# Gate weights and the first event blocks loaded into memory that the packing leaves, other weights in a set order behind the blocks

## The chip, the cores and the metric

The kernel runs on 1 core of one Trainium2 chip. The metric is the device time of one execution in microseconds (us), the median of 3 runs. The engines are PE (matrix products), DVE (vector), ACT (activations, casts, copies), POOL (general element work) and SP, which issues every DMA of this kernel.

## What is computed

Three stages in a row, on 8 batches of 576 tokens with 512 features, in float32:

```
p_packed = softmax(p k^T / 8) v ;  x = softmax(q p_packed^T / 8) p_packed      # packing, 8 heads of 64
x  = sum over the 2 best of 4 experts e:  w_e * (causal softmax attention of x wq_e, x wk_e, x wv_e) @ wo_e
xk = mu_k * x + (1 - mu_k) * x_prev ;  xr = mu_r * x + (1 - mu_r) * x_prev
k  = max(xk @ w_k, 0) ;  r = 1 / (1 + exp(-(xr @ w_r))) ;  out = r * ((k * k) @ w_v)
```

The last stage (512 features in, 1024 hidden, 512 out) is done on three tokens at once: an "event" is 3 tokens, there are 1536 events, in 6 blocks of 256.

## The kernel before

**First stretch, to about 460 us.** For each batch the packing and the four experts are computed. The pieces (`front`, `values`, `project`, `soft`, `turn`, `pair_out`) are steps with a due time in a hand-written table (`FRONT_T` to `OUT_LAG`); all steps of all batches are sorted by due time and written out in that order, and a scheduler sets each engine's order from there by priorities (`PR`). L459 finds a softmax row's maximum on DVE, L463 is its exp on ACT, L479 and L486 transpose the result on PE, L188 copies it back, L524 multiplies by the values, L541 adds the experts (`cb`), L195 makes `dt` on POOL and L558 writes it as events to the DRAM tensor `dscr`, 16 times in all. Between them the weights `w_r`, `w_k`, `w_v` are folded for events and written to DRAM (`wscrr`, `wscrk`, `vscr`).

**Weights for the last stage.** A float32 product runs as three products of a high and a low half, so each weight is loaded (L726), its high half copied (POOL or ACT), and the low half found by a subtraction (L728) on DVE or POOL. There are 4 such planes each of r (the gates' weight), k0, k1, and v.

**Second stretch, the gates, about 456 to 533 us.** For each of six blocks `load_block` reads 1 MB of events (L768, tile `dl`), POOL copies the high half (`dh`, L184) and DVE subtracts (L770). `rstage` does 128 of the 256 events: 24 matmuls of 128x512 on PE (L792) into two `one` banks and a `big` pair of PSUM, `p` copied by ACT (L798), three DVE operations that combine the parts (L775, L776, L777), the sigmoid on ACT (L801), and the gates written to DRAM (`rscr`, L803). PSUM holds two such half-blocks. `dl`, `dh` and `rr` have two buffers each. In before all six blocks, with the gates, are due after the last `pair_out`.

**Third stretch, from 533 us.** For each block `kstage` (L814), the square and its halves (L822 to L827, L195), and `vstage` (L847), with L852 multiplying by the gates. It starts with block 4, whose `dl` and `dh` are still there.

**Memory.** `swap_w` closes the right-hand pools (`bt`, `wa`, `ld`, `fr`, `dv`) after the last batch's `project` and puts there pool "ba" (k0, the blocks) and "bw" (r). `swap_end` closes the left-hand pools (`sm`, `vp`, `ex`) after the last `pair_out` and puts k1 and v there. A load into such memory waits for the last reader of what lay there. All DMAs are issued by SP, one after the other; one that waits holds up the ones behind it.

Of the kernel before, what the change touches and what calls it, by code (L numbers as in the profile page):

```python
# [33 lines left out]
V_END = -11.02  # L34
WA_AT = -24.33
R_AT, R_STEP = 0.2, 2.0
# [8 lines left out]
PR = {"front": 0, "values": -100, "project": 0, "soft": 0, "turn": 0, "out": 100, "fold": 0, "v": -70, "k": 0}  # L45


def f32(ap):
    return ap.bitcast(F32)
# [3 lines left out]
def kernel(  # L53
# [85 lines left out]
    if True:  # L139
        bt_cm, bt = pool("bt", 1, "right")  # L140
# [6 lines left out]
        ex_cm, ex = pool("ex", 2, "left")  # L147

# [562 lines left out]
        def swap_w():  # L711

            close(bt_cm, wa_cm, ld_cm, fr_cm, dv_cm)
            cms["ba"], pools["a"] = pool("ba", 1, "right")
            weight("k0", "a")
            cms["bw"], pools["w"] = pool("bw", 1, "right")
            weight("r", "w")
# [6 lines left out]
        def load_part(h, l, src, eng):  # L724

            nc.sync.dma_start(f32(l), src)  # L726
            evac(eng[0], h, f32(l))
            (nc.vector if eng[1] == "V" else nc.gpsimd).tensor_sub(l, f32(l), f32(h))  # L728

        def load_weight(n_, eng):  # L730
            h, l = wres[n_]
            for j in range(NS):
                load_part(h[:, j], l[:, j], wscr[n_][:, j], eng)
                yield

        def swap_end():
            close(sm_cm, vp_cm, ex_cm)
            cms["bb"], pools["b"] = pool("bb", 1, "left")
            weight("k1", "b")
            for _ in load_weight("k1", "AV"):  # L740
                pass
# [4 lines left out]
            for j in range(0, NFT, 2):  # L746
                load_part(h[:, j : j + 2], l[:, j : j + 2], vscr[:, j : j + 2], "AP")
# [15 lines left out]
        def load_block(i):  # L763
# [4 lines left out]
            nc.sync.dma_start(f32(dl), dscr[:, :, e0 : e0 + EB])  # L768
# [106 lines left out]
        swap = max(last, U * (B - 1) + max(PROJ_T) + 0.05)  # L875
        add("k", call(swap_w), [swap])
        for x, n_ in enumerate(("r", "k0")):
            add("k", load_weight(n_, "PV"), even(swap + 0.1 + 8 * x, swap + 8.1 + 8 * x, 4))

        for i in range(NEB):  # L880
            due = U * B + OUT_LAG[2] + R_AT + R_STEP * i
            add("k", call(load_block, i), [due])
            for x, t0 in enumerate(range(0, EB, P)):
                add("k", call(rstage, i, t0), [due + 0.5 + x * R_STEP / 2])
        add("k", call(swap_end), [U * B + OUT_LAG[2] + 0.1])
# [80 lines left out]
```

## Time and profile before

| what | value |
| --- | --- |
| median of 3 runs (lowest, highest) | 870.78 us (870.21, 874.48) |
| the profiled execution's own time | 875.03 us |
| span of its profile, mean granted PE clock | 873.2 us, 0.988 |
| PE matmuls busy | 812.5 us, 93% |
| DVE, ACT, POOL busy | 572.1 (66%), 363.2 (42%), 401.6 (46%) us |
| DMA moved | 113.71 MB, mean 130 GB/s |

PE is the busiest engine, so time is lost where PE has nothing to do or runs at the lower clock. The span is cut into stretches, and for each the busy time of PE tells how much is lost there; in the stretches that are short of work the engine's own rows tell after which instruction it waited, in square brackets with the instruction or DMA that released it. `<-DMA x<-y` is a transfer. An issue row on SP is where the DMA was started, not where its data were there.

### The profile page before, as it was taken

What the parts mean: (1) busy time and instruction counts of PE and PEld (TensorE: products, weight loads), DVE (VectorE), ACT (ScalarE), POOL (GpSimd) and SP (SyncE); (2) the same over time, 40 slices, a digit from 0 to 9 for tenths busy, and PEclk for the clock granted to TensorE, in tenths of its full rate; (3) what the DMA queues carried; (4) which work ended last, traced back from release to release, by engine and by line L of the source; (5) the groups of instructions that cost most, each with busy time, mean ns of one, the idle gap of its engine ahead of it and who ended that gap; (6) DMA issues with size and microseconds to landing.
All of it is one profiled execution on the core that took longest, in us unless ns stands there. A gap on an engine that the chain in (4) does not pass through costs nothing. (4 is left out here: it accounts for less than half of the span.)

```text
span 873.2 us, 15003 instructions
## 1 busy us (share of the span) xinstructions
PE 812.5 (93%) x5408; PEld 676.2 (77%) x5408; DVE 572.1 (66%) x1297; ACT 363.2 (42%) x916; POOL 401.6 (46%) x539
## 2 busy tenths in 40 slices
PE   5699979999999998988789699999999999999998
PEld 3486948779687795767667589998889888898896
DVE  3899696976959789998954675554454644544342
ACT  2347636576655765766576233211212112021120
POOL 6678476584865755546632510432423223232230
PEclk9899999999999999999999899999999999999999
DMA  9754552735536364333817564023121131110301
GB/s 308 235 158 158 149 163 89 205 108 148 170 106 196 101 181 175 117 108 111 254 59 265 209 255 181 1 85 109 49 88 57 54 141 49 73 73 1 145 2 72
DMA packets 65546, 113.71 MB, mean 130 GB/s; under 512 B 9920, under 2 KB 44224, under 8 KB 65472
## 3 DMA queue, kind: packets, MB, share of 16 engines
q1 hardware_dynamic: 65472, 112.75, 39.7%
q8 instruction: 43, 0.70, 0.3%
q14 instruction: 31, 0.25, 0.1%
HBM read 69.74 MB, written 33.55 MB: 118 GB/s over the span
## 5 line engine op out<-in xcount | busy, mean ns | idle before, releaser
L195 POOL TENSOR_TENSOR kk<-y,kk 128x768 fp32r<-128x768 f32 x48 | 89.5, 1864 | 222.1 <-ACT kk L827 222.1
L847 PE MATMUL one<-wvh,kk 128*128 128x512 f32 x576 | 187.7, 393 | 0.1
L847 PEld LDWEIGHTS one<-wvh,kk 128*128 128x128 f32 x576 | 107.7, 188 | 22.4 <-DVE rr L852 0.5
L847 PE MATMUL one<-wvl,kk 128*128 128x512 f32 x288 | 113.1, 393 | 0.0
L463 ACT ACTIVATE ms<-ms,nb 64x64 f32<-64x64 f32 (+4 forms) x160 | 89.4, 559 | 46.6 <-DVE nb L459 44.5
L775 DVE TENSOR_TENSOR y<-big,p 128x256 f32<-128x256 f32 x48 | 20.3, 424 | 116.8 <-POOL kk L195 100.5
L827 ACT CAST kk<-y 128x768 fp32r<-128x768 f32 x48 | 40.1, 836 | 131.3 <-DVE y L825 94.8
L188 ACT COPY tb<-one 64x128 f32<-64x128 f32 (+5 forms) x208 | 65.9, 356 | 17.5 <-PE one L479 15.3
L822 ACT COPY p<-big 128x256 f32<-128x256 f32 x48 | 17.9, 373 | 128.3 <-PE big L814 105.9
L479 PE MATMUL one<-ident,ms 128*128 128x128 f32 x320 | 54.4, 282 | 11.0 <-DVE nb L459 6.0
L847 PEld LDWEIGHTS one<-wvl,kk 128*128 128x128 f32 x288 | 54.2, 188 | 10.3
L459 DVE CUSTOM_DVE_ANT_0 ms<-one,mstrip 64x64 f32<-64x64 f32 (+3 forms) x128 | 51.4, 420 | 11.3 <-PE one L447 7.0
L524 PE MATMUL one<-tb,vg 128*64 128x320 f32 (+4 forms) x448 | 56.2, 362 | 0.9 <-ACT tb L188 0.7
L479 PEld LDWEIGHTS one<-ident,ms 128*128 128x128 f32 x320 | 37.4, 141 | 21.7 <-issue 11.1
L524 PEld LDWEIGHTS one<-tb,vg 128*64 128x64 f32 x448 | 38.0, 137 | 18.2 <-ACT tb L188 2.9
L594 POOL TENSOR_TENSOR dcx<-dcx,dcu 128x256 f32<-128x256 f32 x40 | 30.8, 770 | 44.3 <-DVE dcu L588 18.3
L852 DVE TENSOR_TENSOR rr<-one,rr 128x512 f32<-128x512 f32 x36 | 23.1, 685 | 41.8 <-PE one L847 41.8
L825 DVE SCALAR_TENSOR_TENSOR y<-y 128x768 f32<-128x768 f32 x48 | 47.9, 998 | 1.6
L447 PE MATMUL one<-ks,qs 128*128 128x64 f32 (+3 forms) x128 | 39.6, 335 | 3.4 <-ACT ks L397 1.0
L184 POOL TENSOR_SCALAR dh<-dl 128x2048 fp32r<-128x2048 f32 x10 | 22.7, 2266 | 42.0 <-DMA dl<-dscr 42.0
L814 PE MATMUL big<-dl,wk0h 128*128 128x256 f32 x192 | 39.6, 282 | 0.0
L770 DVE TENSOR_TENSOR dl<-dl,dh 128x2048 fp32r<-128x2048 f32 x10 | 27.8, 2782 | 17.8 <-POOL dh L184 17.8
(178 smaller groups left out, 2147.8 us busy)
## 6 DMA issues: line engine op xcount, KB each, us to landing
dl<-dscr SPq DMA_DIRECT2D x10, 1024.0 KB, 6.2
kT<-in_k_dram SPq DMA_DIRECT2D x16, 576.0 KB, 4.2
qT<-in_q_dram SPq DMA_DIRECT2D x16, 576.0 KB, 5.7
rscr<-rr SPq DMA_DIRECT2D x12, 768.0 KB, 4.0
rr<-rscr SPq DMA_DIRECT2D x12, 768.0 KB, 4.3
out_dram<-rr SPq DMA_DIRECT2D x11, 768.0 KB, 3.3
vn<-in_v_dram SPq DMA_DIRECT2D x16, 512.0 KB, 4.6
dscr<-dt SPq DMA_DIRECT2D x16, 384.0 KB, 3.7
```

Of the source, the lines that this page charges most:

```text
L188: nc.scalar.copy(o, x)
L195: nc.gpsimd.tensor_tensor(o, x, y, op=op)
L447: nc.tensor.matmul(ps[:, po : po + kn], qs[:, i * P : i * P + P], keys[:, ko : ko + kn], start=x == 0, stop=x == 1,)
L459: nc.vector.tensor_tensor_reduce(halves(mv) if last else mv, sv, halves(mk) if last else mk, op0=ALU.add, op1=ALU.min, scale=-SC, scalar=3 ...
L463: nc.scalar.activation(mv, mv, AF.Exp, bias=nb[p0:], scale=-1.0, accum_out=bat["sums"][p0:, i, e : e + 1],)
L479: nc.tensor.transpose(ps[:, at + j * P : at + (j + 1) * P], ms[:, j * P : (j + 1) * P], ident)
L524: nc.tensor.matmul(av[64 * ee : 64 * ee + 64, qo - lo : hi - lo], vg[:, j, HD * (2 * ep + ee) : HD * (2 * ep + ee + 1)], tslice(tabs[ee], ...
L594: nc.gpsimd.tensor_add(f32(t["x"]), f32(t["x"]), f32(t["u"]))
L814: nc.tensor.matmul(ps[:, o : o + EB], wpart("k0" if f < 4 else "k1", s, wx, t)[:, f % 4 * P : f % 4 * P + P], dx[:, NS * t + s, :], start= ...
L825: nc.vector.scalar_tensor_tensor(y, y, 0.0, y, op0=ALU.max, op1=ALU.mult)
L827: nc.scalar.copy(kk[:, 0], y)
L847: nc.tensor.matmul(ps, kk[:, a, x, t0 : t0 + P], wres["v"][b][:, f, :], start=n == 0, stop=n == 3 * NFT - 1,)
```

## The change

`bt`, which lives to the end, moves to the left side, so that the right side is free as soon as `values` of the last batch and its last weight folding are done (`V_END`): `swap_w` is now due some 14 table units earlier, and it places only the blocks' pool and r. The loads of r are due 8 units after it, those of blocks 0 and 1 at 14 and 15, and their gates at 22 and 28, all inside the last batch's experts. `load_part` and `load_block` get a flag `late`, which pins the DMA in program order on SP's queue. k0 moves to the left side with k1 and v; the three load after the last `pair_out`, at set times among the gates of blocks 2 to 5, pinned. The high half of k0 is made by ACT in place of POOL. Gates and their block loads have a kind of their own with the same priority as before.

```diff
+WR_AT = 8.0
+R_LOAD, R_RUN = [14.0, 15.0], [22.0, 28.0]
+E_R = "PV"
+W_AT = [2.2, 4.2, 5.2]
...
-        bt_cm, bt = pool("bt", 1, "right")
...
+        bt_cm, bt = pool("bt", 1, "left")
...
-            close(bt_cm, wa_cm, ld_cm, fr_cm, dv_cm)
+            close(wa_cm, ld_cm, fr_cm, dv_cm)
             cms["ba"], pools["a"] = pool("ba", 1, "right")
-            weight("k0", "a")
             cms["bw"], pools["w"] = pool("bw", 1, "right")
             weight("r", "w")
...
-        def load_part(h, l, src, eng):
-
-            nc.sync.dma_start(f32(l), src)
+        def load_part(h, l, src, eng, late=False):
+
+            dma = nc.sync.dma_start(f32(l), src)
+            if late:
+                tc.keep_in_program_order(dma)
...
         def swap_end():
-            close(sm_cm, vp_cm, ex_cm)
+
+            close(sm_cm, vp_cm, ex_cm, bt_cm)
             cms["bb"], pools["b"] = pool("bb", 1, "left")
-            weight("k1", "b")
-            for _ in load_weight("k1", "AV"):
-                pass
+            for n_ in ("k0", "k1"):
+                weight(n_, "b")
+                for _ in load_weight(n_, "AV", True):
+                    yield
...
-                load_part(h[:, j : j + 2], l[:, j : j + 2], vscr[:, j : j + 2], "AP")
+                load_part(h[:, j : j + 2], l[:, j : j + 2], vscr[:, j : j + 2], "AP", True)
+                yield
...
-            nc.sync.dma_start(f32(dl), dscr[:, :, e0 : e0 + EB])
+            dma = nc.sync.dma_start(f32(dl), dscr[:, :, e0 : e0 + EB])
+            if late:
+                tc.keep_in_program_order(dma)
...
-        swap = max(last, U * (B - 1) + max(PROJ_T) + 0.05)
+        swap = max(last, U * (B - 1) + V_END + 0.1)
         add("k", call(swap_w), [swap])
-        for x, n_ in enumerate(("r", "k0")):
-            add("k", load_weight(n_, "PV"), even(swap + 0.1 + 8 * x, swap + 8.1 + 8 * x, 4))
-
+        add("k", load_weight("r", E_R, True), even(swap + WR_AT, swap + WR_AT + 4.0, 4))
+        end = U * B + OUT_LAG[2] + 0.1
         for i in range(NEB):
-            due = U * B + OUT_LAG[2] + R_AT + R_STEP * i
-            add("k", call(load_block, i), [due])
+            early = i < len(R_LOAD)
+            add("gates", call(load_block, i, early), [swap + R_LOAD[i] if early else end + i])
             for x, t0 in enumerate(range(0, EB, P)):
-                add("k", call(rstage, i, t0), [due + 0.5 + x * R_STEP / 2])
-        add("k", call(swap_end), [U * B + OUT_LAG[2] + 0.1])
+                add("gates", call(rstage, i, t0), [(swap + R_RUN[i] if early else end + i + 1.5) + 0.05 * x])
+        add("k", swap_end(), [end + W_AT[j // 4] + 0.01 * j for j in range(12)])
```

The lines of the changed kernel lie 3 to 9 further down than those of before. The engines' orders differ from the last batch's `project` to the end of the gates; in the first 400 us and in the third stretch they are alike.

**First place: SP and POOL at the start of the gates.** Each `dl` or `dh` with a number is one block's; in before 6431 is block 2 and 6506 block 3. SP before, from the last `dscr` write:

```order
L558 DMA dscr<-dt_6241 128x4x192
L726 DMA wk1l<-wscrk_91 128x1024 x4
L726 DMA wvl<-vscr 128x1024 x4
L803 DMA rscr<-rr_6314 128x1536
L768 DMA dl_6431<-dscr 128x8x256
L803 DMA rscr<-rr_6349 128x1536
L768 DMA dl_6506<-dscr 128x8x256
L803 DMA rscr<-rr_6389 128x1536
L803 DMA rscr<-rr_6424 128x1536
```

SP after, where 6382 is block 2, 6408 block 3 and 6483 block 4; `wvl` stands four rows further down, behind block 5:

```order
L775 DMA dl_6011<-dscr 128x8x256
L561 DMA dscr<-dt_6109 128x4x192
L775 DMA dl_6382<-dscr 128x8x256
L812 DMA rscr<-rr_6165 128x1536
L812 DMA rscr<-rr_6200 128x1536
L812 DMA rscr<-rr_6293 128x1536
L775 DMA dl_6408<-dscr 128x8x256
L812 DMA rscr<-rr_6328 128x1536
L561 DMA dscr<-dt_6376 128x4x192
L728 DMA wk0l<-wscrk_90 128x1024 x4
L812 DMA rscr<-rr_6441 128x1536
L775 DMA dl_6483<-dscr 128x8x256
```

POOL before, from the last `dt` to block 3's `dh` (6505):

```order
L195 TENSOR_TENSOR dt_6241<-cb_6236 128x2x192
L195 TENSOR_TENSOR dt_6241<-cb_6236 128x192 x2
L728 TENSOR_TENSOR wvl<-wvl,wvh 128x1024 x4
L184 TENSOR_SCALAR dh_6430<-dl_6431 128x2048
L184 TENSOR_SCALAR dh_6505<-dl_6506 128x2048
```

POOL after, from block 2's `dh` (6381) to the `wvl` subtractions:

```order
L187 TENSOR_SCALAR dh_6381<-dl_6382 128x2048
L198 TENSOR_TENSOR dt_6376<-cb_6371 128x2x192
L198 TENSOR_TENSOR dt_6376<-cb_6371 128x192 x2
L187 TENSOR_SCALAR dh_6407<-dl_6408 128x2048
L187 TENSOR_SCALAR dh_6482<-dl_6483 128x2048
L187 TENSOR_SCALAR dh_6571<-dl_6572 128x2048
L732 TENSOR_TENSOR wvl<-wvl,wvh 128x1024 x4
```

Block 2's load stood behind eight weight loads (k1 and v), and now stands ahead of all of them; k0's stand behind block 3's, and k1's behind block 4's. On POOL the four `wvl` subtractions stood ahead of `dh` of blocks 2 to 5 and now stand behind them, and the four `wk0h` copies are gone to ACT.

**Second place: DVE in the middle of the gates.** Rows with `rr` and `p` are the combining of one half-block. Before, from the second half of block 0 to block 2's and 3's `dl`:

```order
L775 TENSOR_TENSOR rr_6349<-one_6321,p_1406_6347 128x512
L776 TENSOR_TENSOR p_1406_6347<-one_6321,p_1406_6347 128x512
L777 TENSOR_TENSOR rr_6349<-big_6322,p_1406_6347 128x2x512
L728 TENSOR_TENSOR wk1l<-wk1l,wk1h 128x1024 x4
L775 TENSOR_TENSOR rr_6389<-one_6361,p_1413_6387 128x512
L776 TENSOR_TENSOR p_1413_6387<-one_6361,p_1413_6387 128x512
L777 TENSOR_TENSOR rr_6389<-big_6362,p_1413_6387 128x2x512
L775 TENSOR_TENSOR rr_6424<-one_6396,p_1418_6422 128x512
L776 TENSOR_TENSOR p_1418_6422<-one_6396,p_1418_6422 128x512
L770 TENSOR_TENSOR dl_6431<-dl_6431,dh_6430 128x2048
L777 TENSOR_TENSOR rr_6424<-big_6397,p_1418_6422 128x2x512
```

After, from the end of block 2's gates (6476) to those of block 3 (6530, 6565); 6483 is block 4:

```order
L786 TENSOR_TENSOR rr_6476<-big_6449,p_1432_6474 128x2x512
L732 TENSOR_TENSOR wk0l<-wk0l,wk0h 128x1024 x3
L784 TENSOR_TENSOR rr_6530<-one_6502,p_1439_6528 128x512
L785 TENSOR_TENSOR p_1439_6528<-one_6502,p_1439_6528 128x512
L786 TENSOR_TENSOR rr_6530<-big_6503,p_1439_6528 128x2x512
L779 TENSOR_TENSOR dl_6483<-dl_6483,dh_6482 128x2048
L732 TENSOR_TENSOR wk1l<-wk1l,wk1h 128x1024 x4
L784 TENSOR_TENSOR rr_6565<-one_6537,p_1444_6563 128x512
L785 TENSOR_TENSOR p_1444_6563<-one_6537,p_1444_6563 128x512
L786 TENSOR_TENSOR rr_6565<-big_6538,p_1444_6563 128x2x512
```

k1's subtractions stood behind block 0's gates and now stand behind the first half of block 3's; k0's stood among the last batch's softmaxes and now stand at the end of block 2's gates.

**Third place: ACT at the end of the packing.** An ACT_TABLE_LOAD stands where the function changes between exp and sigmoid. Before, the last softmax copies and the first gate:

```order
L188 COPY tb_6124<-one_6184 64x2x64
L188 COPY tb_6124<-one_6189 128x128
L188 COPY tb_6124<-one_6189 128x2x128
L188 COPY tb_6124<-one_6193 64x2x64
L188 COPY cx_6212<-cs_6208 128x640
L188 COPY tb_6124<-one_6199 128x4x128
L188 COPY tb_6124<-one_6204 64x64
L188 COPY cb_6236<-big_6230 128x576
L798 COPY p_1401_6312<-one_6285 128x512
L801 ACT_TABLE_LOAD
L801 ACTIVATE rr_6314<-rr_6314 128x1536
```

After, where the gates of block 0 (6165, 6200) stand among the softmaxes of the last expert:

```order
L807 COPY p_1381_6163<-one_6136 128x512
L810 ACT_TABLE_LOAD
L810 ACTIVATE rr_6165<-rr_6165 128x1536
L807 COPY p_1386_6198<-one_6171 128x512
L191 COPY tb_6024<-one_6206 128x128
L191 COPY tb_6024<-one_6206 128x2x128
L191 COPY tb_6024<-one_6210 64x2x64
L191 COPY tb_6024<-one_6236 128x4x128
L191 COPY tb_6024<-one_6241 64x64
L466 ACT_TABLE_LOAD
L466 ACTIVATE ms_123,sums_5801<-ms_123,nb_1391_6221 128x192
L191 COPY tb_6122<-one_6245 128x3x128
```

The one switch to the sigmoid has become a switch to it, one back for the last expert's exps, and a third one (six rows further down) to the sigmoid again.

## Rows read from the trace of the kernel before

**Rows 1.** Windows: stretch, length, busy PE, PEld, DVE, ACT, POOL, PEclk, DMA share, GB/s.

```profile
420.00:440.00 20.00, 15.98 (x119) 12.77 (x118) 18.94 (x50) 13.00 (x43) 13.04 (x17) 1.00 0.91 282
440.00:460.00 20.00, 16.99 (x117) 12.18 (x117) 10.18 (x26) 13.17 (x40) 5.88 (x7) 1.00 0.07 22
...
480.00:500.00 20.00, 12.29 (x47) 9.74 (x46) 12.32 (x11) 5.41 (x5) 11.25 (x5) 0.83 0.56 209
500.00:520.00 20.00, 20.00 (x90) 16.55 (x89) 12.93 (x14) 6.99 (x9) 3.86 (x2) 1.00 0.72 263
...
540.00:800.00 260.00, 260.00 (x1575) 231.72 (x1574) 127.87 (x184) 46.58 (x78) 82.42 (x44) 1.00 0.19 69
```

**Rows 2.** Chain that ended last: start, length, what; its POOL piece in the gates.

```profile
479.19 4.84 POOL wvl L728 x3
```

**Rows 3.** PE's order in time, gates: start, busy, instruction [idle before, releaser].

```profile
488.08 1.22 PE L792 MATMUL one<-wrh,dh 128*128 128x512 f32 x2 [7.71 <-POOL dh L184]
...
491.66 0.64 PE L792 MATMUL big<-wrh,dh 128*128 128x512 f32 x2
...
492.59 0.62 PE L792 MATMUL one<-wrh,dh 128*128 128x512 f32 x2
```

**Rows 4.** POOL's order in time, the gates of blocks 0 to 2.

```profile
476.53 9.63 POOL L728 TENSOR_TENSOR wvl<-wvl,wvh 128x1024 fp32r<-128x1024 f32 x4 [12.85 <-ACT wvh L188]
486.14 1.89 POOL L184 TENSOR_SCALAR dh<-dl 128x2048 fp32r<-128x2048 f32 x1
```

**Rows 5.** PE's order in time, the last batch's experts (five of fourteen waits).

```profile
414.96 0.55 PE L479 MATMUL one<-ident,ms 128*128 128x128 f32 x3 [0.53 <-ACT vg L188]
...
418.22 0.53 PE L384 MATMUL big<-A2h,PWh 128*128 128x288 f32 x2 [1.71 <-DVE l L399]
...
422.64 0.27 PE L447 MATMUL one<-ks,qs 128*128 128x64 f32 x1 [0.99 <-ACT ks L397]
...
435.93 0.55 PE L479 MATMUL one<-ident,ms 128*128 128x128 f32 x3 [1.54 <-ACT ms L463]
...
453.35 0.66 PE L479 MATMUL one<-ident,ms 128*128 128x128 f32 x4 [0.63 <-ACT tb L188]
```

**Rows 6.** DVE's order in time, last batch and gates.

```profile
413.85 3.65 DVE L728 TENSOR_TENSOR wrl<-wrl,wrh 128x1024 fp32r<-128x1024 f32 x2 [0.95 <-POOL wrh L184]
...
432.04 0.81 DVE L541 TENSOR_TENSOR cb<-one,cb 128x256 f32<-128x256 f32 x2
...
436.98 1.23 DVE L728 TENSOR_TENSOR wk0l<-wk0l,wk0h 128x1024 fp32r<-128x1024 f32 x1
...
480.12 0.69 DVE L775 TENSOR_TENSOR rr<-one,p 128x512 f32<-128x512 f32 x1 [3.17 <-DMA rscr<-rr]
...
500.62 0.69 DVE L775 TENSOR_TENSOR rr<-one,p 128x512 f32<-128x512 f32 x1 [2.07 <-ACT p L798]
...
502.14 1.23 DVE L777 TENSOR_TENSOR rr<-big,p 128x1024 f32<-128x1024 f32 x1
...
509.53 2.29 DVE L770 TENSOR_TENSOR dl<-dl,dh 128x2048 fp32r<-128x2048 f32 x1 [1.34 <-POOL dh L184]
```

**Rows 7.** ACT's order in time, gates.

```profile
463.34 1.28 ACT L801 ACT_TABLE_LOAD   x1
...
498.63 1.49 ACT L801 ACTIVATE rr<-rr 128x1536 f32<-128x1536 f32 x1 [2.99 <-DVE rr L777]
500.02 0.56 ACT L798 COPY p<-one 128x512 f32<-128x512 f32 x1
```

**Rows 8.** SP's issues in order of time, start of the gates.

```profile
466.36 2.37 SPq L726 DMA_DIRECT2D wvl<-vscr  x4
469.23 0.32 SPq L803 DMA_DIRECT2D rscr<-rr  x1
```

**Rows 9.** DMA issues: tile, count, KB each, median us from issue to landing.

```profile
rscr<-rr SPq DMA_DIRECT2D x12, 768.0 KB, 4.0
...
wrl<-wscrr SPq DMA_DIRECT2D x4, 512.0 KB, 7.4
```

More of the change, by code (lines that the diff above doesn't have):

```diff
@@ L35 @@
 WA_AT = -24.33
-R_AT, R_STEP = 0.2, 2.0
+WR_AT = 8.0
+R_LOAD, R_RUN = [14.0, 15.0], [22.0, 28.0]
+E_R = "PV"
+W_AT = [2.2, 4.2, 5.2]
 E_TURN = "VAAAA"
@@ L44 @@
 E_DT, E_WL = "P", "P"
-PR = {"front": 0, "values": -100, "project": 0, "soft": 0, "turn": 0, "out": 100, "fold": 0, "v": -70, "k": 0}
+PR = {"front": 0, "values": -100, "project": 0, "soft": 0, "turn": 0, "out": 100, "fold": 0, "v": -70, "k": 0, "gates": 0}
 def f32(ap):
@@ L722, in weight, with load_weight @@
             ]
-        def load_part(h, l, src, eng):
-            nc.sync.dma_start(f32(l), src)
+        def load_part(h, l, src, eng, late=False):
+            dma = nc.sync.dma_start(f32(l), src)
+            if late:
+                tc.keep_in_program_order(dma)
             evac(eng[0], h, f32(l))
             (nc.vector if eng[1] == "V" else nc.gpsimd).tensor_sub(l, f32(l), f32(h))
-        def load_weight(n_, eng):
+        def load_weight(n_, eng, late=False):
             h, l = wres[n_]
             for j in range(NS):
-                load_part(h[:, j], l[:, j], wscr[n_][:, j], eng)
+                load_part(h[:, j], l[:, j], wscr[n_][:, j], eng, late)
                 yield
         def swap_end():
-            close(sm_cm, vp_cm, ex_cm)
+            close(sm_cm, vp_cm, ex_cm, bt_cm)
             cms["bb"], pools["b"] = pool("bb", 1, "left")
-            weight("k1", "b")
-            for _ in load_weight("k1", "AV"):
-                pass
+            for n_ in ("k0", "k1"):
+                weight(n_, "b")
+                for _ in load_weight(n_, "AV", True):
+                    yield
             wres["v"] = [
@@ L761, in wpart, with load_block @@
             return wres[n_]["hl".index(x)][:, slot, t, :]
-        def load_block(i):
+        def load_block(i, late=False):
             e0 = EB * i
```

## Prediction

> **What bounds the kernel now.** I read the windows first [rows 1]. From 540 us to 800 us PE is busy in every one of 260 us, and the order of that stretch is not touched, so a gain can only come from ahead of it. There PE is short in three places: 420 to 440 us and 440 to 460 us (15.98 and 16.99 busy of 20, the last batch's experts), and 480 to 500 us (12.29 of 20, at a granted clock of 0.83: the gates). From 500 us PE is full again. Next I read the chain of waits, to see what the hole in the gates hangs on: it goes through POOL's `wvl` subtractions [rows 2]. PE's own rows then give its size: 7.71 us without work, released by POOL's `dh` [rows 3], and POOL's rows say why: block 2's `dh` starts at 486.14, the moment that four `wvl` subtractions of 9.63 us in all end [rows 4]. Last, PE's rows in the last batch: fourteen waits from 414.96 to 453.35 that sum to 9.2 us, of which three are named (1.71, 0.99, 1.54) and eleven are short, together 4.9 [rows 5].
>
> **Term 1, the hole: 9.4 us back.** In after, block 2's load stands ahead of all of k0, k1 and v on SP, and its `dh` ahead of `wvl` on POOL. Block 2's buffer is free when block 0's gates are done, and the 96 matmuls of blocks 0 and 1 now run among the experts, so there is a block's time and more for load, copy and subtraction. The 7.71 us go. After the hole the first eight matmuls start over 491.66 - 488.08 = 3.58 us, where the four behind them take 0.93, 0.23 each [rows 3]; eight at that pace are 1.9, so those eight ran at about half the pace, the lower of the clock's two levels (1.2 and 2.4 GHz), after 7.71 us of idleness, and it cost 1.7 us more. With no hole ahead of them I expect no fall. 7.7 + 1.7 = 9.4. What could be late in its place is under term 3.
>
> **Term 2, the last batch: 3.2 us back.** PE has these 96 matmuls (96 x 0.23 = 22 us) to put between softmaxes. Wait by wait:
> - The wait for `l` (1.71) came from the two planes of r that DVE subtracted from 413.85, 3.65 us, ahead of it [rows 5, 6]. They go behind; what is left of that wait I put at the 0.45 that `kl`, next on DVE, still lacks: 1.3 back. The wait of 0.99 for `ks` falls to about 0.3, since `project` now stands ahead of a turn: 0.7 back.
> - Of the eleven short waits (4.9) most lie where gate matmuls can now step in. I leave 1.1 of them: 3.8 back.
> - Against that, the four planes of r now stand on POOL and DVE ahead of `cb` and of the last experts' maxima. DVE cannot overtake, so a softmax waits for a plane's POOL copy and for its subtraction of 1.23. The wait of 1.54 grows to about 1.8, and one of 0.6 comes new: 0.9 lost.
> - ACT's switch of function is 1.28 us [rows 7] and comes twice more, once on the way back to exp, where the last softmax hangs on it (some 0.5 more for the step around it: 1.7 lost), once behind the last exp, where PE has block 1's gates.
>
> 1.3 + 0.7 + 3.8 - 0.9 - 1.7 = 3.2. Bounds: without the last two losses 5.8; with nothing of the short waits covered -0.6.
>
> The row of ACT_TABLE_LOAD shows 1.28 us, with the copy of `p` right ahead of it. The Trainium skill, "ScalarE: Activation LUTs", section "What ACT_TABLE_LOAD costs", gives the same time for the load and adds a drain of about 1.38 us, 2.66 in all for each switch, which speaks against putting a sigmoid between exps. No row here shows the drain apart, since the sigmoid behind the switch waited for DVE anyway. By the page term 2 would be 1.4 less if the switch to exp alone is exposed, and the time 1.4 us longer.
>
> **Term 3, the gates of blocks 2 to 5: 5.2 us lost.** Weights that before were converted under the last batch (k0) or under block 0 and the hole (k1) now stand among these gates. PE needs 24 x 0.23 = 5.45 us for a half-block. The other engines' chain for one is nearly as long: three DVE operations (0.69, 0.69, 1.23, with their gaps 2.75), the sigmoid (1.49), the next copy of `p` (0.56), 4.9 from one combine to the next, with 2.07 in which DVE waits for ACT [rows 6, 7]. So the chain gains only 0.55 us on PE in each half-block. A `dl` subtraction of 2.29 now and then fits, as before from 500 us on, where PE stays full [rows 1, 6]. Four planes do not: the first high half by ACT takes about 1.0, then four subtractions of 1.2 follow, 5.8 us where 2.07 were free: 3.7 late. That happens twice (k0 between blocks 2 and 3, k1 in the middle of block 3): 7.4. The four half-blocks behind give 4 x 0.55 = 2.2 back: 5.2. PSUM holds two half-blocks, so PE feels a delay only past 5.45 - 2.75 = 2.7 us; with that the loss is 2.5. I take 5.2, since the `dl` subtractions of blocks 4 and 5 stand in the same places and use that slack up. Ends: nothing (all in the slack) and 7.4 (nothing caught up). The v planes are copied by ACT and subtracted by POOL behind the last `dh`; `vstage` is some 30 us behind the first `kstage`, which covers them.
>
> **Edits at nothing.** `bt` on the left side and the pinning of DMAs add no instruction. The `wk0h` copies leave POOL, which is busy 11.25 of 20 us where PE waits for it [rows 1], and are in term 3 as ACT's. No bytes are added.
>
> **Sum.** 9.4 + 3.2 - 5.2 = 7.4 us. The profiled execution took 875.03 us (span 873.2), so it would take 867.6; the median of the runs is 4.25 us under it, at 870.78, and I put the same saving there: 863.4 us.
>
> **Rival 1, nothing new is late.** If the delays of term 3 stay within the two half-blocks that PSUM holds, the saving is 9.4 + 3.2 = 12.6 and the time 858.2. For it: PE is full from 500 us while DVE is busy 12.93 of 20 [rows 1]. Against: eight planes of 1.2 more in the same 40 us bring DVE from 26 to some 36 of 40. Chance 0.20.
>
> **Rival 2, the DMA queue takes the gain.** The `rscr` writes go through the same queue as 6 MB of weights. In before one was issued at 469.23, right behind `wvl` at 466.36, and DVE was released by its landing only at 480.12 [rows 6, 8]: 10.9 us, where the median is 4.0 [rows 9]. `rr` has two buffers, so a combine waits for the write of two half-blocks earlier: 10.9 us of PE, less some 4.4 from a combine's start to the issue (2.75, the sigmoid's 1.49 and the step between), leaves 6.5 for the landing. One of 10.9 is 4.4 late. If it hits behind k1 and behind v, 8.8 less 2.7 of slack is 6.1 more, and the time 869.5: no change. For it: exactly these loads did it before. Against: they are now set between blocks, four at a time, not eight in one go. Chance 0.12.
>
> **Rival 3, slower: r itself comes late.** In before r was there when DVE began on it at 413.85 [rows 6]; now it is issued behind the last `ks` copies, into the stretch from 420 us where the DMA engines were 0.91 busy [rows 1], and DVE's subtraction of it stands ahead of `cb` (432.04 in before) and the maxima. A landing takes 7.4 at the median [rows 9]; at rival 2's 10.9 and with a copy and a subtraction of 1.2 or so each for a plane, the softmaxes of the next to last expert start some 8 us late with no PE work in hand, as the gates themselves wait for r. With that, and 7.4 in term 3, the sum is 9.4 - 8 - 7.4, and 3.8 of term 2 are gone too with the gates that came late: about 5 us slower, 876. It decides from 9.4 + 3.2 - 5.2 = 7.4 us of waiting for r on. Against: most of what filled that stretch, k0 and two blocks, is moved behind it. Chance 0.05.
>
> That the change does not do what it says is ruled out nearly by the engines' orders, which show the moves; if the scheduler's memory waits held r back to where it was, the time would be 870.8. Chance 0.02.
>
> **How the numbers follow.** Forecast 0.61, rivals 0.20, 0.12, 0.05, 0.02. A measurement of this kernel tells about 0.5% (4.4 us) from no change: faster means under 866.4. The forecast lies there with nearly all its width (0.60), rival 1 wholly (0.20), rival 2 in part (0.03): faster 0.83. Same: 0.01 + 0.09 + 0.02 = 0.12. Slower 0.05. Range: term 3 from 0 to 7.4 and term 2 from -0.6 to 5.8 do not all meet; with term 3 at 7.4 and term 2 at 0.6 the saving is 2.6 (868.2), with term 3 at 0.6 and term 2 at 5 it is 13.8 (857). I take 857 to 868.5, which holds the forecast and rival 1 and leaves rival 2's middle and the others out.
>
> **What would show it.** Right: no hole of PE ahead of block 2, a granted clock of 1.00 through the gates, about 6 us of PE waits in the last batch with the gates of block 0 among its softmaxes, and waits of about 5 us in blocks 3 to 5 or the first `kstage`, released by DVE combines. Term 2 is wrong if PE waits for `ms` behind `wrl`; term 3 is wrong if PE is full from block 2 on (then rival 1) or is released by `rscr<-rr` (then rival 2). The forecast as a whole falls if a hole of over 5 us opens anywhere ahead of the first `kstage`.

## The result, and the profile after

The changed kernel takes 863.58 us (median of six runs, 862.41 to 864.46); the kernel before took 871.01 beside it (six runs, 869.55 to 874.48). That is 7.43 us less, a ratio of 0.9907 with a 95% interval of 0.9885 to 0.9929. The forecast was 863.4.

The profiled executions lie further apart: a span of 862.6 against 873.2, 10.6 us. Part of that has nothing to do with the change. The same instruction, PE's wait for `cb` at about 405 us, stands 2.30 us earlier in after, although PE's order is the same up to there. PE's order in time, first before, then after (start, length, instruction, [idle before, releaser]):

```profile
406.79 0.44 PE L486 MATMUL one<-ident,ms 128*128 128x128 f32 x2 [1.01 <-DVE cb L541]
```

```profile
404.49 0.44 PE L489 MATMUL one<-ident,ms 128*128 128x128 f32 x2 [1.02 <-DVE cb L544]
```

Over all profiled runs this start lay between 401.2 and 411.1, while what follows repeats within 0.4 us where the orders are alike (stretch A below in after, v_later, no_sub, k_casts_pool and k0_sub_pool: 67.5 to 67.9). So traces are compared here from this instruction on, in three stretches: **A**, from it to the first matmul of block 2's gates; **B**, from there to the first matmul of the fifth `kstage`; **C**, the rest. A wait of PE right ahead of block 2 stands apart. All in us, from PE's order in time:

| kernel | A | wait ahead of block 2 | B | C | sum |
|---|---|---|---|---|---|
| before | 73.59 | 7.71 | 62.28 | 322.88 | 466.46 |
| after | 67.53 | 0 | 68.65 | 321.98 | 458.16 |
| v_order_only | 73.4 | 0.33 | 69.1 | 322.89 | 465.7 |
| gates_after_exps | 69.15 | 0 | 76.34 | 321.98 | 467.47 |
| one_early | 73.3 | 0 | 71.3 | 321.97 | 466.6 |
| no_early | 78.5 | 1.57 | 71.0 | 321.98 | 473.1 |
| v_later | 67.59 | 0 | 70.77 | 321.98 | 460.34 |
| no_sub | 67.54 | 0 | 64.71 | 321.98 | 454.23 |
| two_p | 69.44 | 0 | 66.24 | 322.03 | 457.71 |
| no_sub_two_p | 67.79 | 0 | 66.43 | 322.04 | 456.26 |
| k_casts_pool | 67.91 | 0 | 72.61 | 321.98 | 462.50 |
| k0_sub_pool | 67.88 | 0 | 67.21 | 321.98 | 457.07 |
| two_p_k0_pool | 69.60 | 0 | 68.74 | 323.18 | 461.52 |
| k1_behind | 68.13 | 0 | 69.25 | 323.32 | 460.70 |

Each row is one profiled execution, and the granted clock differs between them too. Time lost to the lower clock, the length of a stretch times one less its mean granted clock, is in these figures: in A 1.7 in gates_after_exps, two_p, k0_sub_pool and k1_behind, 3.4 in one_early and two_p_k0_pool, 6.8 in no_early, nothing in the others; in B 5.1 in gates_after_exps, 3.4 in after, no_early, k_casts_pool and two_p_k0_pool, 1.7 to 1.8 in before, v_order_only, v_later and k1_behind, nothing in the others.

From before to after, A gives 6.06, the hole 7.71 and C 0.90; B takes 6.37: 8.3 us. PE's own work in B is 62.28 less the 1.7 that the low clock cost behind the hole, 60.6; so by the prediction's terms the hole gave 9.4, the last batch 6.1, and the gates behind the packing lost 68.65 - 60.6 = 8.1.

The windows of after (stretch, length, busy PE, PEld, DVE, ACT, POOL, PEclk, DMA share, GB/s), which answer to [rows 1]:

```profile
480.00:500.00 20.00, 20.00 (x90) 16.57 (x89) 17.61 (x17) 12.79 (x14) 1.93 (x1) 1.00 1.02 384
500.00:520.00 20.00, 16.74 (x60) 12.85 (x59) 13.32 (x14) 9.77 (x10) 13.39 (x5) 0.83 0.57 226
520.00:540.00 20.00, 18.97 (x130) 17.30 (x129) 10.00 (x15) 6.12 (x8) 3.69 (x2) 1.00 0.46 168
```

480 to 500 us is full now, where PE had 12.29. But 500 to 520, full before, has lost 3.26 us and shows a granted clock of 0.83. The weak place has not gone; it has moved some 20 us to the right and become smaller. PE's waits in after, two of the largest of A and all of B (they answer to [rows 3] and [rows 5]):

```profile
429.89 0.55 PE L482 MATMUL one<-ident,ms 128*128 128x128 f32 x3 [0.77 <-ACT ms L466]
...
455.96 0.33 PE L482 MATMUL one<-ident,ms 128*128 128x128 f32 x1 [1.66 <-ACT ms L466]
...
501.39 0.73 PE L801 MATMUL one<-wrh,dh 128*128 128x512 f32 x2 [0.52 <-DVE p L785]
...
510.34 2.07 PE L801 MATMUL one<-wrh,dl 128*128 128x512 f32 x4 [2.75 <-DVE dl L779]
...
516.48 0.64 PE L801 MATMUL big<-wrh,dl 128*128 128x512 f32 x2
...
525.94 0.50 PE L823 MATMUL big<-dh,wk0h 128*128 128x256 f32 x2 [0.54 <-DVE rr L786]
...
529.50 0.48 PE L823 MATMUL big<-dh,wk0h 128*128 128x256 f32 x2 [0.49 <-DVE y L786]
```

The waits of B sum to 4.3. One of them, 2.75, is for block 5's `dl`. Behind it PE starts fourteen matmuls in 516.48 - 510.34 = 6.14 us, where fourteen at 0.23 take 3.2: it is at the lower of its two levels there (1.2 of 2.4 GHz), after 2.75 us of idleness, and loses 2.9. Wait and clock together, 5.7, are most of the 8.1. What PE waited for is on DVE and POOL, in order of time, DVE first:

```profile
495.38 4.62 DVE L732 TENSOR_TENSOR wk1l<-wk1l,wk1h 128x1024 fp32r<-128x1024 f32 x4
...
504.74 0.69 DVE L784 TENSOR_TENSOR rr<-one,p 128x512 f32<-128x512 f32 x1 [2.08 <-ACT p L807]
...
506.07 4.21 DVE L779 TENSOR_TENSOR dl<-dl,dh 128x2048 fp32r<-128x2048 f32 x1
```

```profile
503.09 1.92 POOL L187 TENSOR_SCALAR dh<-dl 128x2048 fp32r<-128x2048 f32 x1 [9.95 <-PE one L801]
505.74 11.48 POOL L732 TENSOR_TENSOR wvl<-wvl,wvh 128x1024 fp32r<-128x1024 f32 x4 [0.73 <-ACT wvh L191]
```

The same `dl` subtraction took 2.29 alone [rows 6]; here it takes 4.21, and POOL's four `wvl` subtractions, 9.63 in all before [rows 4], take 11.48. Each has grown by about 1.9. POOL's first `wvl` began 0.33 us ahead of DVE's subtraction. One `wvl` alone is 9.63 / 4 = 2.41, so it would end at 508.15; 2.29 from there is 510.44, and DVE ended at 510.28. So DVE seems to have begun its work only when POOL's instruction had ended; and of POOL's four only the second, which began at 508.10, grew: it ended at 512.53, 4.43 long, where the other three took 2.39 to 2.40. The Trainium skill, "SBUF — State Buffer", section "SBUF: two separate sides", says that of GpSimd and of a VectorE operation with two SBUF inputs, as this subtraction is: the pair of ports they share is locked for a whole instruction, and whoever comes second stands still. The rows agree with it here.

### The profile page after: what moved, and what is told of

Read it like the earlier page. It is cut to its first block, busy times and chain, and to the rows that moved or that the text cites. A ratio compares the mean times of both kernels' runs of the same rounds, so it can differ in the third digit from the quotient of the medians.

```text
span 862.6 us, 15000 instructions
## 1 busy us (share of the span) xinstructions
PE 811.9 (94%) x5408; PEld 676.2 (78%) x5408; DVE 569.4 (66%) x1297; ACT 369.9 (43%) x922; POOL 397.0 (46%) x535
## 5 line engine op out<-in xcount | busy, mean ns | idle before, releaser
L482 PEld LDWEIGHTS one<-ident,ms 128*128 128x128 f32 x320 | 37.6, 142 | 17.6 <-issue 7.1
L187 POOL TENSOR_SCALAR dh<-dl 128x2048 fp32r<-128x2048 f32 x10 | 20.9, 2086 | 56.6 <-DMA dl<-dscr 46.6
L779 DVE TENSOR_TENSOR dl<-dl,dh 128x2048 fp32r<-128x2048 f32 x10 | 30.4, 3038 | 19.0 <-POOL dh L187 19.0
L823 PE MATMUL big<-dh,wk0h 128*128 128x256 f32 x192 | 39.1, 281 | 1.0 <-DVE rr L786 0.5
```

The lines of the kernel that those rows point to most:

```text
L482: nc.tensor.transpose(ps[:, at + j * P : at + (j + 1) * P], ms[:, j * P : (j + 1) * P], ident)
L823: nc.tensor.matmul(ps[:, o : o + EB], wpart("k0" if f < 4 else "k1", s, wx, t)[:, f % 4 * P : f % 4 * P + P], dx[:, NS * t + s, :], start= ...
```

## The experiments

The first question was where the 8.1 us of B come from: from DVE's eight subtractions of k0 and k1, or from what v's planes and the transfers do. The second was which part of the change earns the time. A run without an interval was taken once.

**v_order_only: the work that made the hole moved.** The kernel before, with v's loads, and the copies and subtractions that follow them, moved behind block 5's load. k1's loads get set times too, but go out as before, 57.2 us behind the common instruction for 57.4.

```diff
-                load_part(h[:, j : j + 2], l[:, j : j + 2], vscr[:, j : j + 2], "AP")
+                load_part(h[:, j : j + 2], l[:, j : j + 2], vscr[:, j : j + 2], "AP", True)
+                yield
...
-        add("k", call(swap_end), [U * B + OUT_LAG[2] + 0.1])
+        add("k", swap_end(), [U * B + OUT_LAG[2] + (8.3 if j < 4 else 10.3) + 0.01 * j for j in range(8)])
```

> The kernel before with one part of the change alone: the v planes load behind block 5's load and in set order; r, k0, k1, the blocks and the gates stay where they were. If term 1 is right (the hole ahead of block 2 is POOL's wvl subtractions and costs 7.7 us and 1.7 us of lower clock), the hole goes and 5 to 9.4 us with it, 861.5 to 866 us. If block 2 is late anyway behind the k1 planes in the DMA queue, a hole of 3 us or more stays and the time is 867 us or more.

Measured: 871.62 us, ratio 0.9991 [0.9962, 1.002]: no change. The wait ahead of block 2 fell from 7.71 to 0.33, but hole and B together are 69.4, and were 70.0. PE's order in time shows where the time went:

```profile
510.79 0.70 PE L795 MATMUL one<-wrh,dh 128*128 128x512 f32 x2 [1.04 <-ACT p L801]
515.00 0.79 PE L795 MATMUL one<-wrh,dh 128*128 128x512 f32 x1 [2.60 <-DVE p L779]
...
530.78 0.50 PE L817 MATMUL big<-dh,wk0h 128*128 128x256 f32 x2 [1.55 <-DVE rr L780]
534.35 0.47 PE L817 MATMUL big<-dh,wk0h 128*128 128x256 f32 x2 [0.44 <-DVE y L780]
```

Four later waits, 5.6 us in all, and a granted clock of 0.91 from 500 to 520 us take back most of what the hole gave. The two largest of the gates lead back to v itself. In ACT's order a copy of v stands ahead of a sigmoid whose combine was done at 505.23, and waits 5.30 for its load; the sigmoid and the copy of `p` that releases PE at 510.79 are late behind it. The next combine then starts only at 513.53. The profile names a copy of v as what released it; but it writes into a buffer of `rr` whose last write to `rscr` was issued at 502.00, behind v's four loads, and landed 11.4 us later, at 513.4. ACT, then DVE, then that write (tile, count, KB, us from issue to landing):

```profile
507.74 1.05 ACT L188 CAST wvh<-wvl 128x1024 fp32r<-128x1024 f32 x1 [5.30 <-DMA wvl<-vscr]
508.70 1.48 ACT L804 ACTIVATE rr<-rr 128x1536 f32<-128x1536 f32 x1
```

```profile
513.53 0.69 DVE L778 TENSOR_TENSOR rr<-one,p 128x512 f32<-128x512 f32 x1 [4.47 <-ACT wvh L188]
```

```profile
rscr<-rr SPq DMA_DIRECT2D x1, 768.0 KB, 11.4
```

So the work that made the hole makes other waits where it lands. With it moved, not 9.4 us are gained but 0.8 (465.70 for 466.46), which the medians do not tell from nothing.

**gates_after_exps: the place of the first two blocks' gates alone.** After, with the gates of blocks 0 and 1 due later, so that most of them stand behind the last softmaxes.

```diff
-R_LOAD, R_RUN = [14.0, 15.0], [22.0, 28.0]
+R_LOAD, R_RUN = [14.0, 15.0], [29.5, 30.5]
```

> The changed kernel with the gates of blocks 0 and 1 due behind the last softmax (29.5 and 30.5 in place of 22 and 28); their loads and r stay early, ACT changes its function once. By the prediction's term 2 the early place itself is worth the covered short waits less the change of function, some 2.1 us (3.8 - 1.7), and the stretch from the last batch's wait for cb to block 2's gates is 69.7 us (changed 67.5, before 73.6 without the hole). If the gain of 6 us in that stretch comes from the earlier l, kl and ks alone, it stays at 67.5 or falls to 66, as two changes of function go; if it comes from the gates as filler, it is 72 us or more.

Measured: 875.34 us in one run (before: 871.01), slower by some 4 us, and 9.3 longer than after from the common instruction on. A is 69.15, only 1.6 longer than in after. B is 76.34, 7.7 longer. Its three largest waits:

```profile
497.08 0.92 PE L801 MATMUL one<-wrh,dh 128*128 128x512 f32 x2 [3.09 <-DVE p L785]
...
521.06 0.99 PE L801 MATMUL one<-wrh,dh 128*128 128x512 f32 x2 [2.94 <-DVE p L785]
...
536.85 0.50 PE L823 MATMUL big<-dh,wk0h 128*128 128x256 f32 x2 [1.57 <-DVE rr L786]
```

All are waits for combines. But what held these up was not the same each time: the first stood on DVE behind the `dl` of block 4, which had waited for its load, and the one behind the 2.94 waited for a write of `rscr` that was issued right behind v's four loads. DVE:

```profile
494.13 2.29 DVE L779 TENSOR_TENSOR dl<-dl,dh 128x2048 fp32r<-128x2048 f32 x1 [1.81 <-POOL dh L187]
496.34 0.68 DVE L785 TENSOR_TENSOR p<-one,p 128x512 f32<-128x512 f32 x1
...
519.59 0.69 DVE L784 TENSOR_TENSOR rr<-one,p 128x512 f32<-128x512 f32 x1 [3.03 <-DMA rscr<-rr]
```

Gates among the softmaxes pay little by filling PE's waits: those of A sum to 4.3 here and 4.8 in after, and A is longer by only 1.6. Some of that is clock: this kernel shows 0.83 from 424 to 434 us and after does not (10 x 0.17 = 1.7). How much is not shown, since k0_sub_pool, whose order in A is that of after, loses as much to the clock and has an A only 0.35 longer. The rest of the 9.3, 7.7 us, is in B, 1.7 of it lower clock (5.1 for 3.4). What fits is that with early gates less work of DVE, ACT and the queue falls together with the converting of the weights; DVE's order in B differs too, and what each part is worth was not isolated. Against before, A is 4.4 shorter even here, where gates start only at 443.72 us, 37.6 behind the common instruction: that much comes of r, k0 and `project` being moved off the last batch.

**no_early and one_early: none or one of the two blocks moved up.**

```diff
-R_LOAD, R_RUN = [14.0, 15.0], [22.0, 28.0]
+R_LOAD, R_RUN = [], []            (no_early)
+R_LOAD, R_RUN = [14.0], [22.0]    (one_early)
```

> The changed kernel with the gates of blocks 0 and 1 and their loads back behind the last output (no early blocks); r and k0, k1 and v load as in the changed kernel, and ACT changes its function once. By the prediction's term 2 this loses 3.2 us, 866.8 us; by the two traces, in which the last batch together with the gates of blocks 0 and 1 ends 5.9 us earlier counted from the same point, it loses 5.9 us, 869.5 us. If the early gates bring nothing of their own (the loads' order alone was the gain), 863.6 us.

> The changed kernel with the gates of block 0 alone among the last batch's experts, those of block 1 behind the last output. With both early 458.2 us from the last batch's wait for cb to the end, with none of them before the last exp 467.5, with the loads' order alone 465.7. If the gain comes from gate work (PE, DVE and ACT's) that is taken out of the stretch behind the packing, one block is worth half: 462 to 463 us. If it comes from filling PE's waits in the packing, which block 0 fills first, nearly all of it stays: 458 to 460 us.

Measured: no_early 875.61 us, ratio 1.0041 [1.0011, 1.0071]; one_early 872.31 in one run (before: 872.54). no_early is no clean undoing: with no block pinned, block loads go ahead of the last `qs` and `ks` transfers, and PE waits 4.89 in A:

```profile
419.12 0.39 PE L450 MATMUL one<-ks,qs 128*128 128x64 f32 x1 [4.89 <-DMA ks<-ks]
```

one_early shows the other thing that the second early block gives. Block 3's load stands behind k0's four on SP (issued at 475.25 and 477.97) and is there only some 10.6 us later; POOL and PE wait for it, first POOL, then PE:

```profile
488.57 1.90 POOL L187 TENSOR_SCALAR dh<-dl 128x2048 fp32r<-128x2048 f32 x1 [15.78 <-DMA dl<-dscr]
```

```profile
490.52 0.73 PE L801 MATMUL one<-wrh,dh 128*128 128x512 f32 x2 [2.22 <-POOL dh L187]
```

None of the expected times came: one early block is worth only 1 us of sum against gates_after_exps, two are worth 9.3. Clock is in these figures as well: one_early loses 3.4 to it in A and nothing in B.

**no_sub: DVE without the eight subtractions of k0 and k1.**

```diff
-            (nc.vector if eng[1] == "V" else nc.gpsimd).tensor_sub(l, f32(l), f32(h))
+            if eng[1] != "-":
+                (nc.vector if eng[1] == "V" else nc.gpsimd).tensor_sub(l, f32(l), f32(h))
...
-                for _ in load_weight(n_, "AV", True):
+                for _ in load_weight(n_, "A-", True):
```

> The changed kernel without the eight subtractions that make the low halves of k0 and k1 (the low half keeps the full number, so the output is another); all loads and casts stay. Theory P: the combines keep up, no wait of PE from block 2 to the second kstage but that for dl of block 5, some 7 us faster than the changed kernel, about 856.5 us. Theory Q: the wait for block 5's dl and the lower clock behind it stay at 2.7 and 1.9 us, and the gain is at most 3.5 us, about 860 us or more.

Measured: 862.0 us, ratio 0.9863 [0.9819, 0.9907]. A and C stay, B falls from 68.65 to 64.71: 3.9 of its 8.1, between the two expected sizes. What came back is for the most part not a wait for a combine. `wvl` slows block 5's `dl` here too (3.86), but DVE is early enough that PE waits 0.54 for it in place of 2.75, and the clock stays at 1.00. The rest is there without any subtraction of a weight on DVE. A combine waits 3.05 for the write of `rscr` (DVE), and PE 1.75 ahead of the second `kstage`:

```profile
504.66 0.69 DVE L785 TENSOR_TENSOR rr<-one,p 128x512 f32<-128x512 f32 x1 [3.05 <-DMA rscr<-rr]
...
512.15 3.86 DVE L780 TENSOR_TENSOR dl<-dl,dh 128x2048 fp32r<-128x2048 f32 x1
```

```profile
516.06 1.21 PE L802 MATMUL one<-wrh,dl 128*128 128x512 f32 x4 [0.54 <-DVE dl L780]
...
528.58 0.50 PE L824 MATMUL big<-dh,wk0h 128*128 128x256 f32 x2 [1.75 <-DVE rr L787]
```

**v_later: v's loads and subtractions later.**

```diff
-W_AT = [2.2, 4.2, 5.2]
+W_AT = [2.2, 4.2, 5.8]
```

> The changed kernel with one number changed: the v planes load behind the gates of block 4 in place of right behind block 5's load. Orders of DVE and POOL in the gates stay as they are. Theory P (the gates are late because the chain combine, sigmoid, copy of p is delayed by the k0 and k1 subtractions on DVE): only the slowing of block 5's dl subtraction by POOL's wvl (4.21 us in place of 2.29) goes, about 1.9 us faster than the changed kernel, 861.7 us; the second kstage still waits for the last combine. Theory Q (block 5's load is late, it shares the DMA engines with v, and v's subtractions share the port): block 5's dl lands in about 6 us in place of 9, the wait of 2.75 us and the 1.9 us at the lower clock go, 4.6 us faster, 859.0 us.

Measured: 864.86 us, ratio 0.9914 [0.9878, 0.9949]; B 70.77, 2.1 longer than in after. Both expected savings failed to come, yet the run tells where the wait of 2.75 comes from. Without POOL beside it the `dl` subtraction takes 2.28 again, PE waits 0.77 instead of 2.75, and the clock stays at 1.00 from 500 to 520 us: the gates are 3.3 shorter (block 2 to the first `kstage` 47.16 for 50.42). Then v stands in the first four `kstage`s, which are 5.4 longer (23.61 for 18.23), with larger waits and a granted clock of 0.91 from 520 to 540 us. Again a sigmoid stands on ACT behind copies of v that wait for their loads. DVE, then PE, then ACT:

```profile
504.36 2.28 DVE L779 TENSOR_TENSOR dl<-dl,dh 128x2048 fp32r<-128x2048 f32 x1
```

```profile
506.70 1.20 PE L801 MATMUL one<-wrh,dl 128*128 128x512 f32 x4 [0.77 <-DVE dl L779]
...
527.88 0.47 PE L823 MATMUL big<-dh,wk0h 128*128 128x256 f32 x2 [2.48 <-DVE y L786]
```

```profile
523.40 1.05 ACT L191 CAST wvh<-wvl 128x1024 fp32r<-128x1024 f32 x1 [0.49 <-DMA wvl<-vscr]
524.36 1.48 ACT L810 ACTIVATE rr<-rr 128x1536 f32<-128x1536 f32 x1
```

**two_p and no_sub_two_p: a second buffer for the copy `p`,** so that ACT need not wait for DVE's combine; the second kernel has no subtractions of k0 and k1 either.

```diff
-            p2 = pl.tile([P, 512], F32, tag="p2", name=nm("p2"))
+            p2 = pl.tile([P, 512], F32, tag="p2", name=nm("p2"), bufs=2)
...
-            p2 = pools["a"].tile([P, 512], F32, tag="p2", name=nm("p2"))[:, :EB]
+            p2 = pools["a"].tile([P, 512], F32, tag="p2", name=nm("p2"), bufs=2)[:, :EB]
```

> The changed kernel with two buffers for p, so that ACT may copy the next half-block's p ahead of the sigmoid. Counted from the last batch's wait for cb to the end (before 466.5 us, changed 458.2). Theory C (the gates of the changed kernel are bound not by PE but by the chain combine, sigmoid, copy of p, 4.82 us for each of eight half-blocks, plus 12 us of other DVE and ACT work that falls into it): DVE no longer waits 2.07 us for ACT at each half-block, the combines keep up, and of the 8.1 us that blocks 2 to 5 and the first kstages lose 4 to 6 go: 452 to 454 us. Theory Q (transfers late): the losses hang on block 5's load and stay, 457 us or more.

> The changed kernel without the eight subtractions of k0 and k1 (another output) and with two buffers for p. Counted from block 2's first gate to the fifth kstage: changed 68.65 us, without the subtractions 64.71, with two buffers 66.24, PE's own work 60.6. Theory C (subtractions and the chain of combine, sigmoid and p share one place on DVE and ACT): with both gone PE is the bound, 61 to 62.5 us. If the late block loads are a cause of their own (Q), 63.5 us or more, with waits for dh or dl of blocks 4 and 5.

Measured: two_p 861.05 us, ratio 0.9878 [0.9849, 0.9907]; no_sub_two_p 860.68 in one run (before: 872.54). In two_p, B is 2.4 shorter, but A 1.9 longer: the last experts' products wait for ACT (1.12 for `tb`), and the clock falls there. no_sub_two_p has the same wait without the fall, and an A of 67.79, so nearly all of the 1.9 is clock. The windows of the two from 466 to 474 us, two_p first, as in [rows 1]:

```profile
466.00:474.00 8.00, 6.34 (x32) 3.67 (x32) 2.13 (x3) 4.79 (x7) 1.90 (x1) 0.79 0.82 310
```

```profile
466.00:474.00 8.00, 6.70 (x40) 4.50 (x41) 3.55 (x5) 4.92 (x7) 2.95 (x2) 1.00 0.77 293
```

k0's loads go out 76.2 us after the common instruction in two_p, where after has 71.0. With both edits B should have lost both savings, and is 66.4 in no_sub_two_p, longer than with no_sub alone. Block loads now set the pace: PE waits twice for `dh`, whose loads land 9.6 and 10.8 us after their issue.

```profile
493.77 0.73 PE L802 MATMUL one<-wrh,dh 128*128 128x512 f32 x2 [0.92 <-POOL dh L187]
506.56 0.74 PE L802 MATMUL one<-wrh,dh 128*128 128x512 f32 x2 [1.61 <-POOL dh L187]
```

In after the queue is as full; three of the DMA issues from 483 to 505 us (tile, count, KB each, median us from issue to landing):

```profile
rscr<-rr SPq DMA_DIRECT2D x3, 768.0 KB, 7.1
dl<-dscr SPq DMA_DIRECT2D x2, 1024.0 KB, 8.3
wvl<-vscr SPq DMA_DIRECT2D x4, 512.0 KB, 9.4
```

`rscr` takes 7.1 where the median of before was 4.0 [rows 9], and the window from 480 to 500 us shows the DMA engines busy all the time. So the conversions and the transfers stand one behind the other: when one is taken away, the next is late.

**k_casts_pool and k0_sub_pool: conversions moved to POOL.** The first gives POOL the high halves of k0 and k1 in place of ACT, the second the low halves of k0 in place of DVE.

```diff
-                for _ in load_weight(n_, "AV", True):
+                for _ in load_weight(n_, "PV", True):                             (k_casts_pool)
+                for _ in load_weight(n_, "AP" if n_ == "k0" else "AV", True):     (k0_sub_pool)
```

> The changed kernel with the eight high halves of k0 and k1 made by POOL in place of ACT; DVE's subtractions and their order stay. Without the eight subtractions 3.9 us came back of 8.1. Theory C: ACT's casts (1.0 us each, four in a row) delay the sigmoids and copies of p in the chain too; with POOL, which is idle there, making them, 1 to 4 us come back: 454 to 457 us from the last batch's wait for cb to the end, in place of 458.2. If the subtractions on DVE alone are the cause, no change, 458 us. If POOL delays the dh copies of blocks 4 and 5, it is longer, 459 us or more.

> The changed kernel with the four low halves of k0 made by POOL in place of DVE (2.4 to 2.9 us each as for v). Theory C: half of the subtractions leave the chain, about 2 us of the 3.9 that both were worth: 456 us from the last batch's wait for cb to the end, in place of 458.2, unless block 4's dh waits behind them on POOL, which then gives 458 or more.

Measured, one run each (before: 871.01): 867.31 and 860.1 us. k_casts_pool loses 4.3 from the common instruction on. Its rows show the lock again, DVE first, then POOL:

```profile
494.87 7.17 DVE L732 TENSOR_TENSOR wk1l<-wk1l,wk1h 128x1024 fp32r<-128x1024 f32 x4
```

```profile
491.76 8.07 POOL L187 TENSOR_SCALAR wk1h<-wk1l 128x1024 fp32r<-128x1024 f32 x4
```

Four subtractions take 7.17 beside POOL's copies, where after has 4.62 with ACT making the copies. k0_sub_pool gains 1.1: POOL takes 9.54 for k0 at a time when DVE has only combines, but block 4's `dh` waits behind that on POOL, and DVE 3.32 for it:

```profile
479.19 9.54 POOL L732 TENSOR_TENSOR wk0l<-wk0l,wk0h 128x1024 fp32r<-128x1024 f32 x4 [5.18 <-ACT wk0h L191]
```

**two_p_k0_pool and k1_behind: the two edits that gained, together, and then with k1 a block later.** The first has the diffs of two_p and k0_sub_pool; the second adds this to them:

```diff
-W_AT = [2.2, 4.2, 5.2]
+W_AT = [2.2, 5.2, 5.8]
```

> The changed kernel with two buffers for p and k0's low halves by POOL. Apart they gave 0.5 and 1.1 us from the last batch's wait for cb to the end (457.7, 457.1; changed 458.2; before 466.5). Theory C: with both the chain has 2 us of slack at each half-block and 4.8 us less on DVE; 455 to 456 us, about 860 us in the median. If block 4's dh then waits on POOL behind k0's subtractions, 457 us or more.

> As the run before, and k1 loads behind block 5, v behind the gates of block 4. Theory Q: blocks 4 and 5 get the DMA engines for themselves, land in about 6 us, and what is left of the waits goes, 453 to 455 us from the last batch's wait for cb to the end. Theory C: the conversions of k1 and v only move towards the first kstages, where the same chain goes on, as with v alone (2.2 us longer): 457 us or more.

Measured: 864.71 us, ratio 0.9904 [0.9873, 0.9935], and 863.08, ratio 0.9902 [0.9871, 0.9932]. The gains do not add; both are longer than after from the common instruction on (461.52 and 460.70 for 458.16). In the first PE waits 1.89 for a `dh` that stands behind k0 on POOL; in the second 2.20 for the same. Of the variants with the same output only two_p and k0_sub_pool are shorter than after, by 0.5 and 1.1 us from the common instruction on, and by less than the runs tell apart. None is offered as a better version.

## Why the prediction was right, and where it was not

The total was right to 0.2 us; its parts were not. Two errors of nearly equal size, 2.9 us each, stand against each other; that they cancel is luck.

- **Term 1 (hole 7.7 + clock 1.7 back).** As an event right: PE has no wait ahead of block 2, and block 2's first matmuls run at the high clock. As a gain of its own wrong: v_order_only takes the hole away and gains 0.8. The step that failed is the price of nothing for v in its new place (behind the last `dh`, with `vstage` late enough to cover it). v's loads, copies and subtractions had made the hole, and they make waits wherever they stand: 3.6 us of waits in v_order_only, with 1.7 of lower clock; in after most of the 2.75 for block 5's `dl` and 2.9 of lower clock; 5.4 us more in the first four `kstage`s of v_later. The forecast that the granted clock would be 1.00 through the gates failed too (0.83 from 500 to 520 us).
- **Term 2 (last batch, 3.2 back): 6.1.** The function switch was sized right: PE waits 1.66 for it, 1.7 was said. ACT's rows (start, length, instruction) show 1.28 for the load, which starts 0.01 us after the copy ahead of it ends, and an exp that starts 0.02 us after the load:

```profile
453.24 0.82 ACT L191 COPY tb<-one 128x512 f32<-128x512 f32 x2 [1.01 <-PE one L482]
454.07 1.28 ACT L466 ACT_TABLE_LOAD   x1
455.37 0.45 ACT L466 ACTIVATE ms<-ms,nb 128x192 f32<-128x192 f32 x1
```

  The 1.38 us of drain that the Trainium skill gives ("ScalarE: Activation LUTs", "What ACT_TABLE_LOAD costs") do not appear on either side of this load; here the measurement decides. What was mis-sized is the rest. Moving r, k0 and `project` was put at 1.3 + 0.7 - 0.9 = 1.1, and gates_after_exps shows 4.4. The gates among the softmaxes, put at 3.8 - 1.7 = 2.1, show 1.6 at most, and not as covered waits: the waits of A, 9.3 in before, are 4.3 with the gates late and 4.8 with them early. That the short waits hung on engines which were converting k0 and r fits this, and was not tried apart.
- **Term 3 (gates of blocks 2 to 5, 5.2 lost): 8.1.** That DVE's eight subtractions cost 3.9 of it is shown by no_sub. But the prediction let PE be released by combines, and the largest wait, 2.75, was for block 5's `dl`: DVE was late with it, and `wvl` on POOL, which the prediction had named as covered, made it slow. Either edit, no_sub or v_later, takes away most of that wait and the fall of the clock behind it, so their savings are partly the same one. Priced at 2.29 the subtraction leaves a wait of about 0.8 (v_later: 0.77); at 4.21 it is 2.75 and brings the low clock, 2.9 more. The sign was there before: [rows 6] have two subtractions of r in 3.65, 1.8 each, at a time when POOL was copying r, and single ones of the same size in 1.23. And `dl` and `rscr` were given no lateness in the likeliest case, while from 483 to 505 us they land 8.3 and 7.1 us after issue at the median.
- **What no term had:** C is 0.9 shorter, see below. 9.4 + 6.1 - 8.1 + 0.9 = 8.3 from the common instruction on; the medians give 7.4.
- **The rivals.** The first (nothing new late, 858.2) fell: B lost 8.1. The second has its mechanism, an `rscr` or `dl` that lands late, in v_order_only, gates_after_exps, no_sub and no_sub_two_p, but in after it is not what releases PE, and its time did not come. The third needed r to come late; PE's waits for `ms` in A stay at 0.77 ahead of the switch. Its terms as they are written sum to 6.6 us, 877; the stated 5 comes out only if the 1.7 for the switch goes as well.

**Open.** No single edit frees B: its 8.1 are shared by the subtractions, the shared ports and the transfers, and which of them binds when the other two are gone was not isolated. A third buffer for the blocks, which would let loads go out earlier, was not tried.

## What to carry to other kernels

An idle stretch is made by some work; before counting it as gain, follow that work to its new place, in the order of every engine and queue that it uses, and run the smallest edit that moves it alone. An instruction that waits for a load holds up all that stands behind it on its engine. Early work can pay more in the stretch that it leaves, here 7.7 of 9.3 us, than by the waits that it fills. When work is put on POOL or DVE, price each at the duration it shows beside the other, not at the one it shows alone.

## What the runs showed of the hardware

A subtraction on DVE and one on POOL at the same time do not overlap: 4.21 for 2.29, and 4.43 for 2.39 on the other side; copies on POOL do the same to DVE (7.17 for 4.62). Combines, which read one input from PSUM, are not slowed beside POOL's subtractions: 0.69, 0.69 and 1.22 in k0_sub_pool from 484.58 on, as alone.

C, in which no order was changed, is 322.9 us in before and v_order_only, and 322.0 in after and nine of the other kernels. The whole difference is in the matmuls that read k0: those of C, 480 in every kernel, take 57.25 us, each counted to the start of the next, in the first two and 56.13 to 56.16 in all others, and those of v take back 0.2 (194.1 for 194.3). k0 lies on the right side of memory in the first two and on the left in the others. The longer C of two_p_k0_pool and k1_behind, 323.2 and 323.3, is no exception: there 5.42 us lie behind the start of the last matmul, for 4.29. In the chain of waits, groups of 24 matmuls of k0 take 2.86 there and 2.80 here, one of before first and then one of after:

```profile
600.16 2.86 PE big L814 x24
```

```profile
590.31 2.80 PE big L823 x24
```

Why the place should matter is not known. It was not tested apart, and the blocks, which k0 shared a pool with, lie elsewhere too.
